# Attention with hash buckets and a soft mixture of experts: another start-up and other emission times

## Chip, cores and metric

The kernel runs on one core of one Trainium2 chip. The metric is the device time of one execution in microseconds (us). Engines are TensorE (PE, with its weight loads as PEld), VectorE (DVE), ScalarE (ACT), GpSimd (POOL) and SyncE (SP), whose queue issues most transfers.

## What is computed

Four batches of eight heads, 768 positions, 64 columns a head. Every position of q and of k gets a bucket number from the signs of six projections; a score counts only where the buckets agree. What the attention gives goes through a soft mixture of eight experts with four slots each.

```python
q_bits = (np.einsum('bhsd,dk->bhsk', q, proj) > 0)      # k_bits alike
mask   = q_bucket[:, :, :, None] == k_bucket[:, :, None, :]
scores = np.where(mask, scale * np.matmul(q, k.T), -1e9)
attn   = np.exp(scores - np.max(scores, -1, keepdims=True))
attn   = attn / (np.sum(attn, -1, keepdims=True) + 1e-09)
x      = attn @ v                       # then, over (B*S, H*D):
logits = x @ phi                        # dispatch weights: softmax over rows
slot_out = relu(slot_input @ w1) @ w2   # combine weights: softmax over slots
out    = c @ slot_out
```

## The kernel before, in words

**One head.** A tile `XY` holds, on 128 partitions, what the scores of a head are multiplied from: rows 0 to 63 the high part of q and k, rows 64 to 95 the bits and a row of shifts, rows 96 to 127 the low parts. Three such tiles take turns (the names XY_134, XY_135 and XY_136 in the rows are heads 0, 1 and 2, then again). `smax` (L395) multiplies rows 0 to 95 for a first estimate of each row's maximum: 12 pieces a head, which fill nine PSUM tiles, two of them at a time (`p_sm`), and DVE reduces each (L409, L412). `shift` and `shift_rows` (L422 to L441) turn the maxima, ACT casts them (L440), and SP sends them into row 64 of the head's tile (`XY<-mr`). Only then can `scores` (L444) multiply all 128 rows; ACT takes the exponential of each of the nine `st` tiles (L457). POOL adds the exponentials up (`acc`, L464 and L470), and `av` (L472) multiplies them with v.

**A pair of heads.** q and k of two heads come in one load each (`load`, L200: `stage<-qk`, 384 KB each, two of them). `split_hi` (ACT, L307) and `split_lo` (POOL L317 for the first two pairs, then DVE L314) cut them into parts, `bits` (L356) multiplies by the projections and `over` (L347) compares. The `spread_` functions (L324 to L391) copy these into the `XY` tiles with DMAs inside the chip, through SP. The `pair_` functions sum, invert and turn what two heads give; `batch_` functions do the same for eight heads.

**The order.** Nothing is scheduled by a tool: `at` (L754) gives each step a number from the tables ONCE and STEADY (numbers count tiles, 6 a head and 12 a pair; a STEADY number holds for every pair), the steps are sorted by it, and each engine runs its own instructions in the order in which the steps then record them. A pair takes 12 slots, so a slot of the table is a twelfth of a pair's time. Each engine waits only for its own next instruction: what stands behind a waiting one waits too, on SP as well.

**The start.** Before head 0 can begin, `first_bits` (L364) casts q and k, multiplies bits and compares them in four pieces, two of q and then two of k (DVE, L348 through `over`). TensorE is kept at work in between: `keep_warm` (L250) multiplies constants, and `spin` (L416) is a filler of 64 rows by 512 columns of head 0's own tile, four ahead of the first maxima (`at(spin, 4)`) and two after each of head 0's nine maxima (L414).

**The end.** Expert weights are loaded by `load_weights` at numbers of the tables and, in the last 14 slots, as buffers come free; the experts follow behind the last head (from L866).

Of the kernel before, what the change touches and what calls it, by code (L numbers as in the profile page):

```python
# [18 lines left out]
P = 128  # L19
# [26 lines left out]
    ('acc', 0, 0): 3.585914, ('acc', 0, 1): 4.22685, ('acc', 0, 2): 5.524667, ('acc', 1, 0): 8.946979,  # L46
    ('acc', 1, 1): 10.956391, ('acc', 1, 2): 12.344873, ('av', 0, 0): 5.054363, ('av', 0, 1): 5.478537,
    ('av', 0, 2): 5.757673, ('av', 1, 0): 9.710007, ('av', 1, 1): 10.255163, ('av', 1, 2): 11.214499,
# [3 lines left out]
    ('pair_add', 0): 17.755806, ('pair_log', 0): 17.093498, ('pair_rec', 0, 0): 16.439496,  # L52
    ('pair_rec', 0, 1): 17.493222, ('pair_rec', 0, 2): 17.06204, ('pair_sum', 0): 14.253612,
    ('pair_turn', 0): 15.311115, ('pair_x', 0, (0, 1)): 20.048062, ('pair_x', 0, (2,)): 17.817429,
    ('scores', 0, 0, 0): 0.168486, ('scores', 0, 0, 1): 1.125661, ('scores', 0, 1, 0): 1.223956,
    ('scores', 0, 1, 1): 0.33384, ('scores', 0, 2, 0): 2.334467, ('scores', 0, 2, 1): 2.987076,
    ('scores', 0, 3, 0): 3.245695, ('scores', 0, 3, 1): 0.44555, ('scores', 0, 4, 0): 3.495737,
    ('scores', 0, 4, 1): 2.875345, ('scores', 0, 5, 0): 3.003256, ('scores', 0, 5, 1): 4.099239,
    ('scores', 1, 0, 0): 6.858146, ('scores', 1, 0, 1): 5.870022, ('scores', 1, 1, 0): 5.92247,
    ('scores', 1, 1, 1): 6.192369, ('scores', 1, 2, 0): 8.409656, ('scores', 1, 2, 1): 7.415615,  # L60
    ('scores', 1, 3, 0): 7.420621, ('scores', 1, 3, 1): 8.585449, ('scores', 1, 4, 0): 8.877145,
    ('scores', 1, 4, 1): 8.735371, ('scores', 1, 5, 0): 8.835046, ('scores', 1, 5, 1): 7.918247,
    ('shift', 0): -3.784083, ('shift', 1): 2.753538, ('shift_rows', 0): -2.475046, ('shift_rows', 1): 4.45141,
    ('smax', 0, 0, 0): -5.130492, ('smax', 0, 0, 1): -8.590815, ('smax', 0, 1, 0): -7.560504,
    ('smax', 0, 1, 1): -7.539257, ('smax', 0, 2, 0): -8.690095, ('smax', 0, 2, 1): -6.037478,
    ('smax', 0, 3, 0): -5.866639, ('smax', 0, 3, 1): -5.350979, ('smax', 0, 4, 0): -3.977164,
    ('smax', 0, 4, 1): -4.372204, ('smax', 0, 5, 0): -4.147594, ('smax', 0, 5, 1): -6.133271,
    ('smax', 1, 0, 0): 0.789461, ('smax', 1, 0, 1): -2.662486, ('smax', 1, 1, 0): -2.516273,
    ('smax', 1, 1, 1): 0.351061, ('smax', 1, 2, 0): 0.154013, ('smax', 1, 2, 1): 2.575717,
    ('smax', 1, 3, 0): 2.715207, ('smax', 1, 3, 1): 0.080615, ('smax', 1, 4, 0): 2.254769,  # L70
    ('smax', 1, 4, 1): -3.276176, ('smax', 1, 5, 0): -2.661486, ('smax', 1, 5, 1): 1.386723,
    ('split_hi', 0): -19.520063, ('split_lo', 0, 0): -13.277774, ('split_lo', 0, 1): -14.899121,
    ('spread_bits', 0): -12.730307, ('spread_bits', 1): -6.105477, ('spread_l', 0): -3.252795,
    ('spread_l', 1): -6.507778, ('spread_x', 0): -6.522482, ('spread_x', 1): -2.692262, ('spread_y', 0): -12.855738,
    ('spread_y', 1): -7.587243,
# [17 lines left out]
    ('load_weights', 6): 88.324917, ('load_weights', 7): 94.440496, ('load_weights', 8): 100.324917,
    ('load_weights', 9): 106.440496, ('one_add', 30): 190.865, ('one_add', 31): 193.725, ('one_fold', 3): 189.99,
    ('one_log', 30): 188.431, ('one_log', 31): 193.7, ('one_put', 30): 191.5, ('one_put', 31): 195.722,
    ('one_rec', 30): 190.86, ('one_rec', 31): 192.8, ('one_sum', 30): 189.395, ('one_sum', 31): 191.0,
    ('one_turn', 30): 189.777, ('one_turn', 31): 192.0, ('one_x', 30): 191.23, ('one_x', 31): 193.72,
    ('scores', 10, 0, 1): 61.076546, ('scores', 12, 0, 1): 73.076546, ('scores', 14, 0, 1): 85.076546,
    ('scores', 16, 0, 1): 97.076546, ('scores', 18, 0, 1): 109.076546, ('scores', 20, 0, 1): 121.076546,
    ('scores', 3, 2, 0): 20.32086, ('scores', 5, 2, 0): 32.32086, ('scores', 6, 0, 1): 37.076546,  # L100
    ('scores', 7, 2, 0): 44.32086, ('scores', 8, 0, 1): 49.076546, ('scores', 9, 2, 0): 56.32086,
    ('shift_rows', 0): -3.190102, ('smax', 1, 0, 0): 1.271144, ('smax', 1, 0, 1): 1.233474,
    ('smax', 1, 1, 0): 1.270655, ('smax', 1, 1, 1): -2.856536, ('smax', 1, 2, 0): -1.78673,
    ('smax', 1, 2, 1): -0.694624, ('smax', 1, 3, 0): -0.199892, ('smax', 1, 3, 1): 0.329768,
    ('smax', 1, 4, 0): 0.343642, ('smax', 1, 4, 1): -2.830546, ('smax', 1, 5, 0): -2.805791,
    ('smax', 1, 5, 1): -2.024059, ('spin', 0): -35.655358, ('split_hi', 2): -28.475173, ('split_lo', 0, 0): -33.5,
    ('split_lo', 0, 1): -32.0, ('split_lo', 2, 0): -28.344955, ('split_lo', 2, 1): -3.110769,
    ('spread_bits', 1): -29.5, ('spread_bits', 2): 0.979704, ('spread_l', 0): -33.0, ('spread_l', 1): -3.111769,
    ('spread_l', 2): 3.432598, ('spread_x', 0): -31.0, ('spread_x', 1): -21.308377, ('spread_x', 2): 9.432814,
    ('spread_y', 1): -34.0, ('spread_y', 2): 0.523129, ('spread_y', 25): 136.325917, ('spread_y', 27): 148.325917,  # L110
    ('spread_y', 29): 160.325917, ('spread_y', 3): 4.325917, ('spread_y', 31): 172.325917,
# [35 lines left out]
def lsh_attention_soft_moe(  # L147
# [61 lines left out]

    eps = cp.tile([P, 1], F32, name="eps")  # L210
# [3 lines left out]
    ones = cp.tile([P, 32], F32, name="ones")  # L214
    nc.vector.memset(ones, 1.0)
    idle = pts[2][:, 0:P]
    nc.vector.memset(idle, 1.0)
# [145 lines left out]

    def first_bits():  # L364
        w = parts_of(0)
        bt = st[0]["bt"] = st[1]["bt"] = pp.tile([P, HC], F32R, name="bt", bufs=1)
        for x in range(2):
            pt = p_st.tile([P, 512], F32, name="st")
            bits_of(0, x, pt)
            nc.scalar.copy(Ys[0][0:64, x], raw[0:64, x])  # L370
            if x == 0:
                nc.scalar.copy(w[:, 0], raw[:, 0])
            for j in (2 * x, 2 * x + 1):
                over(Ys[0][64:80, x, (j % 2) * HC:(j % 2 + 1) * HC], pt, slice(32 * j, 32 * j + 16))
            if x:
                nc.scalar.copy(pts[0][0:64, 0:HC], before[0:64, 0:HC])
                nc.scalar.copy(w[:, 2], raw[:, 1])
                nc.scalar.copy(pts[0][64:128, 0:HC], pt[64:128, 0:HC])
            before = pt
# [681 lines left out]
```

## Time and profile before

| what | value |
|---|---|
| three runs | 494.96, 500.72, 505.84 us (median 500.72) |
| the profiled execution | 495.73 us, of which the span of its instructions is 493.9 us |
| busy share of the span | PE 97%, PEld 60%, DVE 74%, ACT 50%, POOL 67% |
| mean granted TensorE clock | 0.97 of full speed |
| chain that ended last | PE 87%, DMA 9%, DVE 1% |
| DMA | 99.71 MB, mean 202 GB/s |

The table is one execution. A stretch of the span is read from the time at which the first instruction named in it starts. The full clock is 2.4 GHz; where a row says 0.50, the granted one is 1.2 GHz.

### The profile page before, as it was taken

How to read it: one execution, taken by the hardware profiler on the slowest of the kernel's cores; microseconds unless marked ns; L12 is line 12 of the kernel's file. 1: busy time of each engine (PE TensorE's matmuls, PEld its weight loads, DVE VectorE, ACT ScalarE, POOL GpSimd, SP SyncE). 2: the span in 40 equal slices, each digit the busy share in tenths (PEclk: the TensorE clock that was granted, in tenths of full speed). 3: DMA queues.
4: the chain of work that ended last, by engine and by line, in shares of the span. 5: the costliest groups of instructions: out<-in, count | busy, mean ns of one | idle time of the engine just before them, and what ended most of it. 6: DMA issues, size and time to landing. Idle time of an engine off the chain costs nothing.

```text
span 493.9 us, 10762 instructions
## 1 busy us (share of the span) xinstructions
PE 477.1 (97%) x4047; PEld 298.8 (60%) x4047; DVE 367.1 (74%) x690; ACT 246.3 (50%) x465; POOL 331.1 (67%) x236
## 2 busy tenths in 40 slices
PE   8999999799999999999999999999999999989992
PEld 6466666465666566656566666666666665553581
DVE  3466888487989897978899988888889866463242
ACT  5127464345566546554666464646565544531251
POOL 8619686578777796868677968686779687702200
PEclk9569999899999999999999999999999999999997
DMA  6646675848575756676775777767767578999967
GB/s 153 152 117 153 164 165 151 200 93 225 119 224 122 202 141 165 180 209 178 195 188 170 191 209 183 208 178 212 181 184 173 153 171 286 376 353 406 409 248 286
DMA packets 39696, 99.71 MB, mean 202 GB/s; under 512 B 7422, under 2 KB 13708, under 8 KB 39644
## 3 DMA queue, kind: packets, MB, share of 16 engines
q1 hardware_dynamic: 39260, 98.16, 69.0%
q0 software_dynamic: 224, 0.47, 0.4%
q8 instruction: 32, 0.52, 0.4%
q10 hardware_dynamic: 160, 0.39, 0.3%
q14 instruction: 20, 0.16, 0.1%
HBM read 52.76 MB, written 6.29 MB: 120 GB/s over the span
## 4 chain that ended last, share of the span: by engine, by line
PE 87%; DMA 9%; DVE 1%; SPq 0%; issue 0%; ACT 0%; DVEq 0%; ACTq 0%
PE st L453 27%; PE av L482 22%; PE smx L406 15%; DMA XY<-mr 5%; PE qs L974 3%; PE qh L892 3%; DMA stage<-qk 2%; PE mi L494 2%; PE mi L544 2%; PE mi L353 2%; PE av L420 2%; DMA w<-w 2%; PE mi L509 1%; PE mi L529 1%; PE mi L699 1%; PE qa L937 1%
## 5 line engine op out<-in xcount | busy, mean ns | idle before, releaser
L470 POOL TENSOR_TENSOR acc<-acc,pt 128x768 f32<-128x768 f32 x125 | 229.2, 1833 | 37.1 <-ACT pt L457 29.5
L457 ACT ACTIVATE pt<-st 128x512 f32<-128x512 f32 x288 | 162.4, 596 | 57.5 <-PE st L453 50.3
L453 PE MATMUL st<-XY 128*128 128x512 f32 (+1 forms) x768 | 172.0, 345 | 4.3 <-DMA XY<-mr 4.2
L412 DVE TENSOR_REDUCE mx<-smx 128x1 f32<-128x512 f32 x192 | 130.4, 687 | 36.2 <-PE smx L406 33.7
L482 PE MATMUL av<-pt,v 128*32 128x384 f32 x1536 | 137.0, 488 | 0.0
L453 PEld LDWEIGHTS st<-XY 128*128 128x128 f32 x768 | 121.9, 192 | 19.5 <-DMA XY<-mr 5.6
L406 PE MATMUL smx<-XY 96*128 96x512 f32 (+1 forms) x384 | 124.2, 372 | 0.5 <-DVE mx L412 0.5
L464 POOL TENSOR_TENSOR acc<-pt 128x768 f32<-128x768 f32 x32 | 58.8, 1837 | 49.9 <-ACT pt L457 49.7
L406 PEld LDWEIGHTS smx<-XY 96*128 96x128 f32 x384 | 69.8, 195 | 33.0 <-DVE mx L412 8.3
L482 PEld LDWEIGHTS av<-pt,v 128*32 128x32 f32 x1536 | 46.6, 110 | 67.6 <-issue 66.7
L409 DVE TENSOR_REDUCE mx<-smx 128x2 f32<-128x512 f32 x96 | 63.8, 677 | 11.4 <-PE smx L406 10.7
L486 ACT COPY avs<-av 128x384 f32<-128x384 f32 x32 | 15.3, 478 | 93.9 <-PE av L482 93.9
L314 DVE TENSOR_REDUCE stage<-stage 128x768 fp32r<-128x1536 f32 x28 | 50.2, 1792 | 1.0 <-ACT pt L457 0.4
L501 DVE RECIPROCAL sm<-sm 128x128 f32<-128x128 f32 x45 | 39.7, 912 | 0.0
L546 DVE TENSOR_TENSOR xq<-mi,r 128x256 f32<-128x256 f32 x45 | 17.5, 418 | 24.3 <-PE mi L544 24.3
L307 ACT ACTIVATE stage<-stage 128x768 fp32r<-128x768 f32 x30 | 24.5, 839 | 17.8 <-DMA stage<-qk 12.9
L544 PEld LDWEIGHTS mi<-ident,avs 128*128 128x128 f32 x90 | 10.5, 141 | 11.4 <-issue 9.4
L974 PE MATMUL qs<-w 128*32 128x128 f32 (+1 forms) x360 | 15.8, 305 | 0.0
L544 PE MATMUL mi<-ident,avs 128*128 128x128 f32 x90 | 15.6, 281 | 0.0
L931 POOL CAST avs<-lacc 128x48 fp32r<-128x48 f32 x8 | 2.1, 268 | 19.5 <-ACT lacc L922 12.4
L892 PE MATMUL qh<-w,siT 128*32 128x512 f32 x128 | 14.6, 595 | 0.0
L353 PE MATMUL mi<-stage,pb 128*32 128x384 f32 x120 | 13.1, 510 | 0.0
(179 smaller groups left out, 346.6 us busy)
## 6 DMA issues: line engine op xcount, KB each, us to landing
w<-w SPq DMA_DIRECT2D x61, 512.0 KB
XY<-stage SPq DMA_DIRECT2D x62, 384.0 KB
stage<-qk SPq DMA_DIRECT2D x32, 384.0 KB
XY<-stage SPq DMA_DIRECT2D x62, 192.0 KB
v<-vt SPq DMA_DIRECT2D x32, 192.0 KB
out<-w SPq DMA_DIRECT2D x12, 512.0 KB
xq<-w SPq DMA_DIRECT2D x3, 512.0 KB
XY<-bt SPq DMA_DIRECT2D x62, 19.5 KB
```

Of the source, the lines that this page charges most:

```text
L314: nc.vector.tensor_reduce(out=w[:, 2 * x + 1], in_=stage[:, x:n + 1:n - x].rearrange("p t s -> p s t"), axis=AX.X, op=ALU.add, negate=True)
L406: nc.tensor.matmul(pt[:, o:o + b - a], Ys[h % N_Y][0:96, 0, t * P:(t + 1) * P], Ys[h % N_Y][0:96, 1, a:b], start=True, stop=True)
L409: nc.vector.tensor_reduce(out=mx[:, n - 1:n + 1], in_=pt.rearrange("p (a x) -> p a x", a=2), axis=AX.X, op=ALU.max)
L412: nc.vector.reduce_max(out=mx[:, n:n + 1], in_=pt, axis=AX.X)
L453: nc.tensor.matmul(pt[:, o:o + b - a], x[:, 1, i * P:(i + 1) * P], x[:, 0, a:b], start=first, stop=not first)
L457: nc.scalar.activation(pts[i // 2][:, 512 * u:512 * u + 512], pt, AF.Exp, scale=D ** -0.5)
L464: nc.gpsimd.tensor_tensor(out=s["acc"], in0=pr[:, 0:S], in1=pr[:, S:2 * S], op=ALU.add)
L470: eng.tensor_tensor(out=s["acc"], in0=s["acc"], in1=pr[:, a * S:(a + 1) * S], op=ALU.add)
L482: nc.tensor.matmul(s["av"][D * c + d:D * c + d + 32, 0:HC], s["v"][:, i, d:d + 32], pr[:, o + c * HC:o + (c + 1) * HC], start=(i == 0), st ...
L501: nc.vector.reciprocal(out=rs[:, k * P:(k + 1) * P], in_=rs[:, k * P:(k + 1) * P])
L544: nc.tensor.transpose(pt[:, o:o + P], st[h + a]["avs"][:, k * P:(k + 1) * P], ident)
L974: nc.tensor.matmul(po[32 * j:32 * j + 32], hTs[g][:, f, 32 * j:32 * j + 32], wt[1, x, 2 * g + f // 4, j].rearrange("p (f m) -> p f m", f=4 ...
```

## The change

1. The start: the two memsets that the first constant matmuls need go to the front of DVE. SP issues k, then the constants with the projections, then q (before: constants, q, k).
2. `first_bits` works on k first. Of the four comparisons three stand ahead of the first maximum (both of k, the first of q); the fourth, with the two copies out of PSUM, is a step of its own (`first_last`) behind it.
3. Fillers: `spin` covers 96 rows in place of 64 and is issued once in place of twice behind each maximum of head 0; the four ahead of them are gone; `keep_warm` ahead of them goes from 14 to 3.
4. New numbers for nearly all steps, in both tables.

```diff
-    def load(h):
-        for x in range(2):
+    def load(h, xs=(0, 1)):
+        for x in xs:
             nc.sync.dma_start(out=raw[:, x], in_=qk[x, h // 2])
...
+    load(0, (1,))
     nc.sync.dma_start(out=pre[:, 0:C_ID + 64], in_=first[:, 0:C_ID + 64])
-    load(0)
+    load(0, (0,))
...
+    def first_over(x, c):
+        j = 2 * x + c
+        over(Ys[0][64:80, x, c * HC:(c + 1) * HC], first_pt[x], slice(32 * j, 32 * j + 16))
+
     def first_bits():
         w = parts_of(0)
-        for x in range(2):
-            pt = p_st.tile([P, 512], F32, name="st")
-            bits_of(0, x, pt)
-            nc.scalar.copy(Ys[0][0:64, x], raw[0:64, x])
-            if x == 0:
-                nc.scalar.copy(w[:, 0], raw[:, 0])
-            for j in (2 * x, 2 * x + 1):
-                over(Ys[0][64:80, x, (j % 2) * HC:(j % 2 + 1) * HC], pt, slice(32 * j, 32 * j + 16))
...
+        for x in (1, 0):
+            first_pt[x] = p_st.tile([P, 512], F32, name="st")
+            bits_of(0, x, first_pt[x])
+            nc.scalar.copy(Ys[0][0:64, x], raw[0:64, x])
             if x:
                 nc.scalar.copy(w[:, 2], raw[:, 1])
+                first_over(1, 0)
+                first_over(1, 1)
+        first_over(0, 0)
+        nc.scalar.copy(w[:, 0], raw[:, 0])
+
+    def first_last():
+        first_over(0, 1)
+        nc.scalar.copy(pts[0][64:128, 0:HC], first_pt[1][64:128, 0:HC])
+        nc.scalar.copy(pts[0][0:64, 0:HC], first_pt[0][0:64, 0:HC])
...
         if h == 0 and n % 4 != 1:
-            spin(2)
+            spin(1)
...
-        y = Ys[0][0:64, 0]
+        y = Ys[0][0:96, 0]
...
-    at(keep_warm, 14, True, tag="a")
+    at(keep_warm, 3, True, tag="a")
     at(copy_ident)
     at(first_bits)
+    at(first_last)
...
-    at(spin, 4, tag=0)
...
-    ('bits', 0): -13.111727, ('load', 0): -19.876778, ('load_v', 0): 0.438592, ('load_v', 1): 6.200893,
+    ('bits', 0): -13.641611, ('load', 0): -22.629268, ('load_v', 0): -2.150801, ('load_v', 1): 1.001645,
```

**TensorE at the start.** `av<-pt_84` are the constant matmuls of `keep_warm`, `st<-stage` the bits of head 0, `av<-XY_134` the fillers, `smx<-XY_134` the pieces of head 0's maxima. Before:

```order
L254 MATMUL av<-pt_84,ones 32x128 x7
L353 MATMUL st<-stage,pb 32x384 x4
L254 MATMUL av<-pt_84,ones 32x128 x14
L420 MATMUL av<-XY_134 128x512 x4
L406 MATMUL smx<-XY_134 128x512
L420 MATMUL av<-XY_134 128x512 x2
L406 MATMUL smx<-XY_134 128x256 x2
```

After the change:

```order
L258 MATMUL av<-pt_84,ones 32x128 x7
L357 MATMUL st<-stage,pb 32x384 x4
L258 MATMUL av<-pt_84,ones 32x128 x3
L418 MATMUL smx<-XY_134 128x512
L432 MATMUL av<-XY_134 128x512
L418 MATMUL smx<-XY_134 128x256 x2
L432 MATMUL av<-XY_134 128x512
```

Fifteen matmuls fewer stand between the bits and the first piece of a maximum, and one filler in place of two behind each piece.

**SP's queue around the row of maxima of head 5** (`XY_136<-mr`), the third pair of heads. `w<-w` are expert weights, `stage<-qk` the loads of a later pair, `XY<-stage` and `XY<-bt` copies inside the chip. Before:

```order
L293 DMA v_88<-vt 128x384
L189 DMA w<-w 128x1024 x2
L202 DMA stage<-qk 128x768 x2
L321 DMA XY_135<-stage 64x2x768
L321 DMA XY_136<-mr 1x12x128
L321 DMA XY_134<-stage 64x2x768
```

After the change:

```order
L297 DMA v_89<-vt 128x384
L205 DMA stage<-qk 128x768 x2
L192 DMA w<-w 128x1024 x2
L325 DMA XY_136<-mr 1x12x128
L325 DMA XY_135<-stage 64x2x768
L325 DMA XY_135<-bt 13x384 x2
```

The copy of 64 by 2 by 768 now stands behind the row of maxima, the loads of q and k stand ahead of the weights, and a load of v comes right ahead of these; the later pairs have the same order with one weight load.

**POOL in a pair of the steady stretch.** `acc` are the sums of a head's exponentials, out of the three buffers pt_82, pt_83 and pt_84; `lacc` is the sum of the pair before's logits. Before:

```order
L464 TENSOR_TENSOR acc_86<-pt_82 128x768
L470 TENSOR_TENSOR acc_86<-acc_86,pt_83 128x768 x2
L470 TENSOR_TENSOR acc_86<-acc_86,pt_84 128x768 x2
L523 TENSOR_TENSOR lacc<-lacc,sm 128x384
L464 TENSOR_TENSOR acc_87<-pt_82 128x768
```

After the change:

```order
L476 TENSOR_TENSOR acc_86<-pt_82 128x768
L482 TENSOR_TENSOR acc_86<-acc_86,pt_83 128x768 x2
L535 TENSOR_TENSOR lacc<-lacc,sm 128x384
L482 TENSOR_TENSOR acc_86<-acc_86,pt_84 128x768 x2
L476 TENSOR_TENSOR acc_87<-pt_82 128x768
```

The sum of logits has moved ahead of the last two sums of exponentials.

## Rows read from the trace of the kernel before

**Rows 1.** Busy time by stretch: length, five engines, granted clock, DMA share, GB/s.

```profile
10.75:25.19 14.44, 14.44 (x31) 6.69 (x30) 6.22 (x9) 2.98 (x4) 9.90 (x9) 0.60 0.64 146
...
48.88:73.42 24.54, 24.54 (x208) 15.75 (x211) 20.99 (x37) 13.49 (x26) 18.36 (x11) 1.00 0.67 165
73.42:103.07 29.65, 26.37 (x208) 17.04 (x211) 21.21 (x37) 13.58 (x26) 19.27 (x12) 0.94 0.72 174
103.07:128.40 25.33, 24.80 (x207) 15.78 (x211) 20.81 (x37) 13.58 (x26) 19.30 (x12) 1.00 0.63 162
...
203.62:228.54 24.92, 24.82 (x208) 15.81 (x211) 21.15 (x37) 13.61 (x26) 19.32 (x12) 1.00 0.69 192
228.54:253.76 25.22, 24.81 (x208) 15.80 (x211) 21.16 (x37) 14.00 (x27) 18.00 (x12) 1.00 0.71 184
...
328.97:353.50 24.53, 24.53 (x207) 15.74 (x211) 21.44 (x37) 13.94 (x27) 18.02 (x12) 1.00 0.72 197
...
432.11:441.74 9.63, 8.37 (x93) 4.91 (x94) 6.16 (x25) 2.72 (x8) 0.04 (x1) 1.00 0.95 376
```

**Rows 2.** The chain that ended last, start and us, at the start.

```profile
10.82 0.43 PE smx L406
11.25 0.66 PE av L420 x2
...
21.83 0.72 PE smx L406 x2
22.55 1.15 PE av L420 x2
...
44.31 0.47 PE st L453 x2
...
44.78 0.24 PE smx L406
```

**Rows 3.** Instructions in order of time, all engines, 0 to 31 us: start, us.

```profile
6.10 2.76 DVE L348 TENSOR_SCALAR XY<-st,con 16x384 fp32r<-16x384 f32 x4 [3.19 <-PE st L353]
...
10.75 0.50 PE L406 MATMUL smx<-XY 96*128 96x512 f32 x1
...
11.29 0.69 DVE L412 TENSOR_REDUCE mx<-smx 128x1 f32<-128x512 f32 x1 [2.43 <-PE smx L406]
...
18.09 0.84 ACT L307 ACTIVATE stage<-stage 128x768 fp32r<-128x768 f32 x1 [1.33 <-DMA stage<-qk]
...
25.19 0.17 DVE L427 TENSOR_REDUCE mi<-mx 128x6 f32<-128x12 f32 x1
...
25.50 1.51 PE L353 MATMUL mi<-stage,pb 128*32 128x384 f32 x8
...
27.46 0.26 ACT L440 CAST mr<-mi 12x128 fp32r<-12x128 f32 x1 [8.52 <-PE mi L437]
27.74 0.81 SPq L321 DMA_DIRECT2D XY<-mr  x1
...
30.80 0.63 PE L453 MATMUL st<-XY 128*128 128x512 f32 x1
```

**Rows 4.** Instructions in order of time, SP and TensorE, 82 to 95 us.

```profile
82.63 0.85 SPq L202 DMA_DIRECT2D stage<-qk  x2
...
85.64 0.69 SPq L321 DMA_DIRECT2D XY<-stage  x1
...
86.71 0.77 SPq L321 DMA_DIRECT2D XY<-mr  x1
...
94.83 0.74 PE L453 MATMUL st<-XY 128*128 128x256 f32 x4 [3.28 <-DMA XY<-mr]
```

**Rows 5.** Instructions in order of time, POOL and DVE, 340 to 350 us.

```profile
340.85 7.58 POOL L470 TENSOR_TENSOR acc<-acc,pt 128x768 f32<-128x768 f32 x4 [1.67 <-ACT pt L457]
...
344.79 0.56 DVE L521 TENSOR_TENSOR sm<-mi,sm 128x384 f32<-128x384 f32 x1
...
348.39 1.02 POOL L523 TENSOR_TENSOR lacc<-lacc,sm 128x384 f32<-128x384 f32 x1
```

More of the change, by code (lines that the diff above doesn't have):

```diff
@@ L53 @@
[L53 to L58, printed above, removed]
@@ new lines @@
+    ('pair_add', 0): 17.577879, ('pair_log', 0): 16.993927, ('pair_rec', 0, 0): 15.693025,
+    ('pair_rec', 0, 1): 15.7677, ('pair_rec', 0, 2): 15.521381, ('pair_sum', 0): 14.239421,
+    ('pair_turn', 0): 15.346973, ('pair_x', 0, (0, 1)): 20.437414, ('pair_x', 0, (2,)): 17.890042,
+    ('scores', 0, 0, 0): 0.095393, ('scores', 0, 0, 1): 1.201587, ('scores', 0, 1, 0): 2.467216,
+    ('scores', 0, 1, 1): 0.576418, ('scores', 0, 2, 0): 0.194762, ('scores', 0, 2, 1): 2.954077,
+    ('scores', 0, 3, 0): 3.066209, ('scores', 0, 3, 1): 2.808786, ('scores', 0, 4, 0): 2.713342,
@@ new lines @@
+    ('scores', 0, 4, 1): 3.452949, ('scores', 0, 5, 0): 4.612255, ('scores', 0, 5, 1): 0.740437,
+    ('scores', 1, 0, 0): 6.224469, ('scores', 1, 0, 1): 6.596277, ('scores', 1, 1, 0): 6.933339,
+    ('scores', 1, 1, 1): 6.295257, ('scores', 1, 2, 0): 7.197935, ('scores', 1, 2, 1): 7.034394,
+    ('scores', 1, 3, 0): 7.126508, ('scores', 1, 3, 1): 9.279904, ('scores', 1, 4, 0): 9.595666,
+    ('scores', 1, 4, 1): 8.443296, ('scores', 1, 5, 0): 9.009943, ('scores', 1, 5, 1): 7.777135,
+    ('shift', 0): -3.732058, ('shift', 1): 2.981046, ('shift_rows', 0): -2.48744, ('shift_rows', 1): 4.460206,
@@ new lines @@
+    ('load', 10): 37.688669, ('load', 12): 49.688669, ('load', 14): 61.688669, ('load', 2): -12.762070462,
+    ('load', 4): 3.305061249, ('load', 6): 13.688669, ('load', 8): 25.688669, ('load_phi',): 10.931086823,
+    ('load_v', 0): -61.78673, ('load_weights', 0): 26.669343, ('load_weights', 1): 27.9087,
+    ('load_weights', 10): 111.216379, ('load_weights', 11): 119.361725, ('load_weights', 12): 123.216379,
+    ('load_weights', 13): 131.361725, ('load_weights', 14): 135.216379, ('load_weights', 15): 143.361725,
@@ new lines @@
+    ('one_add', 30): 190.865, ('one_add', 31): 193.725, ('one_fold', 3): 189.99, ('one_log', 30): 188.431,
+    ('one_log', 31): 193.7, ('one_put', 30): 191.5, ('one_put', 31): 195.722, ('one_rec', 30): 190.86,
+    ('one_rec', 31): 192.8, ('one_sum', 30): 189.395, ('one_sum', 31): 191.0, ('one_turn', 30): 189.777,
+    ('one_turn', 31): 192.0, ('one_x', 30): 191.23, ('one_x', 31): 193.72, ('scores', 10, 0, 1): 61.396684,
+    ('scores', 12, 0, 1): 73.396684, ('scores', 14, 0, 1): 85.396684, ('scores', 16, 0, 1): 97.396684,
@@ new lines @@
+    ('scores', 18, 0, 1): 109.396684, ('scores', 20, 0, 1): 121.396684, ('scores', 3, 2, 0): 19.21665,
+    ('scores', 5, 2, 0): 31.21665, ('scores', 6, 0, 1): 37.396684, ('scores', 7, 2, 0): 43.21665,
+    ('scores', 8, 0, 1): 49.396684, ('scores', 9, 2, 0): 55.21665, ('shift_rows', 0): -3.614750908,
+    ('smax', 0, 0, 0): -48.201477503, ('smax', 1, 0, 0): -0.414889731, ('smax', 1, 0, 1): -0.455916355,
+    ('smax', 1, 1, 0): -0.415889731, ('smax', 1, 1, 1): -2.391596163, ('smax', 1, 2, 0): 1.521154004,
@@ L207, in lsh_attention_soft_moe @@
     vs = [held.tile([P, NT, D], F32, name=f"v{i}") for i, held in enumerate((ap, mp))]
+    ones = cp.tile([P, 32], F32, name="ones")
+    nc.vector.memset(ones, 1.0)
+    idle = pts[2][:, 0:P]
+    nc.vector.memset(idle, 1.0)
     eps = cp.tile([P, 1], F32, name="eps")
```

96 lines of the change are left out of this document (36 added, 60 removed).

## The prediction, made before the changed kernel ran

> **What bounds the kernel now.** I read the page's shares first (TensorE busy 97% of the span, mean granted clock 0.97), then busy time by stretch, the chain that ended last, and the order of time where the chain leaves TensorE or where the change works. By stretch [rows 1] a pair of heads takes 24.53 or 24.54 us and TensorE is busy in all of it; VectorE has some 3 us to spare there. So in the steady stretch TensorE sets the time, and an order of the same matmuls can hardly win. Time to be won lies where TensorE waits or does filling work:
>
> - The start. Head 0's maxima fill 10.75 to 25.19, 14.44 us for nine reductions, at a mean granted clock of 0.60. The chain shows why [rows 2]: it runs through TensorE's pieces and fillers, not through VectorE. At 10.8 us a piece takes 0.43 us and two fillers 0.66; at 22 us, at the low clock (1.2 GHz), 0.72 and 1.15, 1.87 a step, while a reduction is 0.69 [rows 3]. The fillers are 61% of a step.
> - Four pairs that take longer than 24.54: 29.65, 25.33, 24.92 and 25.22 [rows 1], together 6.96 us more. In the largest the row of maxima is issued at 86.71 and TensorE's first score starts at 94.83 after 3.28 us idle, released by that row [rows 4]; afterwards the clock is low for a while (mean 0.94 of the stretch, busy 26.37 in place of 24.54).
>
> **The change part by part.** All sums are made against the profiled execution, 495.73 us (span 493.9 and 1.83 around it). It lies 5.0 below the median of the three runs, 500.72, and near the lowest.
>
> *Ahead of the first piece.* Now four comparisons run from 6.10 for 2.76 us, 0.69 each, and the first piece starts at 10.75 [rows 3], behind fillers. After the change k and the constants come first, in the place of constants and q: the same bytes, so the bits of k are ready about when those of q are now. Three comparisons end at 6.10 + 3 x 0.69 = 8.17, and the fillers that remain (three constant matmuls) are over by then. The first piece starts near 8.3: 2.4 us won (2.0 to 2.7, as k lands a little later or earlier). The memsets moved on VectorE are worth under 0.1.
>
> *The nine maxima.* The lower end is VectorE's: 0.54 from the first piece to its reduction (11.29 less 10.75), nine reductions and the fourth comparison at 0.69, and some 0.5 because the second filler reads what that comparison writes and the third piece stands behind it: 0.54 + 10 x 0.69 + 0.5 = 7.9. The upper end keeps the low clock and today's cost of a filler: 9 x (0.72 + 1.15 / 2) + 0.5 = 12.2. Between them I take 8.8, nearer to the lower: the 0.43 at full clock is 0.2 more than the 0.235 of each of two scores, and of a piece between scores (0.47 for two, 0.24 for one [rows 2]), so the extra belongs to the change between 64 and 96 rows, which goes. Then 14.44 becomes 8.8, 5.6 won, and the maxima end near 8.3 + 8.8 = 17.1 in place of 25.19.
>
> *What is late next.* The cast of the row of maxima is behind the casts of the second pair's q and k on ACT, and the bits of that pair (four matmuls, in rows 25.50 and 1.51 us [rows 3]) stand ahead of head 1's pieces on TensorE. Both need the second k, which lands at 18.09 now [rows 3]; ACT is free of it at 18.93. So of the 8.0 won so far a part is given back. From the bits at 25.50 to the first score at 30.80 is 5.30 us now, and the row issued at 27.74 has landed by then. With k no earlier the first score stands at 18.09 + 5.30 = 23.4, 7.4 won. One copy of ACT's (32 x 2 x 768 numbers, 0.20 MB, 1.35 us at the 146 GB/s of this stretch [rows 1]) has gone behind the cast of the row. If half of that was ahead of k, the score stands at 22.7, 8.1 won. Bounds: 6.4 (k a microsecond later) to 9.0 (the clock is full and the bits save 0.8 too). I take 8.0. The Trainium skill, DMA: Bandwidth & Descriptors, "Issuing engines are not separate DMA queues", says that transfers from any engine run on the same DMA engines and interleave; by it that copy does count against the load, and without it 7.4 would stand.
>
> What head 1 and head 2 need next is issued in the same order behind this and has slack: SP's transfers for them follow the row at once.
>
> *The row of maxima in the steady stretch.* Ahead of it on SP stands now a copy of 64 x 2 x 768 numbers, 0.39 MB, issued at 85.64, about a microsecond before the row [rows 4]; at the 165 to 174 GB/s of these stretches [rows 1] it takes some 2.3 us. It goes behind the row. That alone is more than the excess of three of the four long pairs (0.79, 0.38, 0.68) and 2.3 of the 5.11 of the first. The loads of q and k, now issued at 82.63, four microseconds ahead, get a number 2.75 slots lower, 2.75 x 24.54 / 12 = 5.6 us earlier, as far as SP's queue allows, which takes the rest. Against it, a load of v (0.20 MB) is now in front. The bounds are 0 won and 6.96; I take 6.0, as the trace has the row late by less than the copy in three cases of four.
>
> *The rest of the steady order.* The matmuls are the same in number and shape. TensorE has no idle time in an undisturbed pair, which hides the moves on VectorE, ACT and POOL; cover can be lost (third rival). I cost it at 0, with 0.2 us a pair either way, 3 us over 15 pairs. The end, with its wait for weights (432.11 to 441.74, DMA share 0.95 [rows 1]), is issued in slots counted from the last head and moves with the loop.
>
> Sum: 495.73 - 8.0 - 6.0 = 481.7, say **482 us**.
>
> **The rivals.**
>
> *The row of maxima stays late.* For it: the change puts weights, v, q and k (about 2 MB) straight ahead of the row; at 376 GB/s, the best rate in these rows, they need 5.3 us, and the runs spread over 11 us, more than the 7 us of waits in the trace. Against it: all of these were ahead of the row before too, and the copy is gone. Then only the start is won: 495.73 - 8 = 488, and 493 with the median run's 5 us more.
>
> *The clock stays low and the fillers cost what they do now.* Fillers are there to hold the clock; the trace lost it with twice as many, while TensorE was busy 14.44 of 14.44 us [rows 1], so halving them cannot be counted on to hold it. The maxima then take 12.2 and the start wins 2.4 + 2.2 = 4.6, with k no longer the last. 495.73 - 4.6 - 6 = 485. The Trainium skill, TensorE: Matmul & The Clock Gate, "Part 1: The HAM clock gate", says that the slow state is the default and activity releases it; by that rule fewer fillers mean more of the slow clock, and this is where it would lead. The stretch at 0.60 does not contradict it.
>
> *POOL comes late (slower).* The sum of logits now stands ahead of the last two sums of exponentials. In the trace the four sums run 340.85 to 348.43, and the logits' product, which POOL's sum waits for, ends at 345.35 on VectorE [rows 5]. Moved ahead, POOL does two sums to 344.6, waits to 345.4, adds 1.02, and ends the other two (1.9 each) at 350.2, 1.7 us later than now. Those two free the buffer pt_84 for the next head's exponentials; beyond that ACT waits, then TensorE, whose three score buffers fill. POOL idles in the pair (18.0 to 19.3 busy of 24.5 [rows 1]) and so catches up, and the exponentials have about a microsecond before TensorE feels them. From a product some 2 us later than now each further microsecond is paid in 11 or 12 pairs. To be slower than 495.73 it must eat 14 us, 1.2 a pair; at 2 us a pair, 482 + 24 = 506. Against it: VectorE's slack.
>
> **How the numbers follow.** Forecast 0.62 (477 to 487), the late row 0.22 (486 to 494), the low clock 0.11 (483 to 488), POOL 0.05 (500 to 510). The range for 8 in 10 reaches from 476 (start 9.0, waits 7.0, order 3 better) to 494. About 2% is what a measurement of this kernel can tell from no change, 490.7 against the median. The forecast gives 0.58 of its 0.62 to faster (against a run of before near 495 it could be less than 2%), the late row half, 0.11, the low clock 0.09, together 0.78; POOL gives 0.04 to slower; the rest, 0.18, is within 2%.
>
> **What would show it right or wrong.** The first piece of a maximum near 8.3; nine reductions with little idle time on VectorE, ending near 17; ACT's second cast of the new k as the last thing ahead of the row's cast; the first score near 22.8. Undisturbed pairs all at 24.5, no wait of TensorE for the row of maxima, DMA's share of the chain down from 9%. Wrong: a first score behind 26, waits for the row of over 3 us in all, pairs of over 25, or ACT waiting for POOL's sums in every pair.

## The result, and the profile after

The changed kernel takes **482.3 us** (median of four runs, 480.1 to 482.8) against 499.1 us before (median of four, 495.0 to 505.8): ratio 0.968, 95% interval 0.960 to 0.976. It is faster, and the prediction was 482, 476 to 494. The profiled execution took 480.1 us, span 478.4. Some executions of a kernel are over 1.5% longer than its fastest, at a lower granted clock: ratios here leave them out, medians do not, and no trace of one is read.

The page of the kernel after: busy shares, and the chain that ended last by engine.

```profile
PE 461.8 (97%) x4012; PEld 290.6 (61%) x4012; DVE 364.4 (76%) x690; ACT 250.3 (52%) x465; POOL 330.5 (69%) x236
...
PE 90%; DMA 2%; POOL 2%; DVE 2%; issue 1%; ACT 1%; SPq 1%; DVEq 0%; ACTq 0%; POOLq 0%
```

TensorE's share is what it was, over a span that is 15.5 us shorter: waits and fillers went together. Transfers, 9% of the chain before, are 2%.

Busy time by stretch after: head 0's maxima, the third pair of heads, and in the last row 14 pairs together (PEclk is TensorE's granted clock as a share of full speed).

```profile
core 0: us, PE busy (x) PEld busy (x) DVE busy (x) ACT busy (x) POOL busy (x), PEclk, DMA share, GB/s
7.93:15.99 8.06, 6.53 (x21) 4.44 (x21) 6.80 (x10) 3.24 (x5) 7.91 (x8) 0.79 0.86 217
...
64.33:88.91 24.58, 24.58 (x204) 15.75 (x203) 20.91 (x37) 13.64 (x26) 18.94 (x12) 1.00 0.76 200
...
39.78:388.73 348.95, 348.95 (x2900) 222.93 (x2899) 300.03 (x529) 197.99 (x366) 272.87 (x164) 1.00 0.70 181
```

The same 14 pairs before:

```profile
48.81:404.12 355.31, 350.99 (x2901) 224.48 (x2900) 301.63 (x529) 194.35 (x366) 272.89 (x164) 1.00 0.68 177
```

Against [rows 1]: the nine maxima take 8.06 us where they took 14.44. The pair that took 29.65 takes 24.58, and the other three long ones are down to 24.6 too; TensorE is busy in all of the 348.95 us. (Every fourth pair, three of the 14, takes 26.1 us in both kernels: 26.12 before, 26.13 to 26.18 after.)

For the rest of the document the span is cut in three: the *start*, up to the first matmul of head 1's weighted sums (48.8 us before, 39.8 after), the *14 pairs* from there to the same matmul of head 29 (355.3 before, 348.95 after), and the *end*, 89.8 and 89.7. The gain of 15.5 us is 9.0 in the start and 6.4 in the pairs.

The start after, in order of time, all engines (rows of before: [rows 3]).

```profile
5.18 1.38 DVE L352 TENSOR_SCALAR XY<-st,con 16x384 fp32r<-16x384 f32 x2 [0.94 <-PE st L357]
...
7.12 0.67 DVE L352 TENSOR_SCALAR XY<-st,con 16x384 fp32r<-16x384 f32 x1 [0.56 <-PE st L357]
...
8.44 0.69 DVE L424 TENSOR_REDUCE mx<-smx 128x1 f32<-128x512 f32 x1 [0.65 <-PE smx L418]
...
8.85 3.59 POOL L321 TENSOR_TENSOR stage<-stage 128x768 fp32r<-128x768 f32 x2
...
12.58 1.65 POOL L352 TENSOR_SCALAR bt<-pt,con 128x384 fp32r<-128x384 f32 x1
...
14.25 3.29 SPq L325 DMA_DIRECT2D XY<-bt  x4
...
17.42 0.84 ACT L311 ACTIVATE stage<-stage 128x768 fp32r<-128x768 f32 x1 [1.74 <-DMA stage<-qk]
...
18.43 0.77 SPq L325 DMA_DIRECT2D XY<-mr  x1
...
19.01 0.70 PE L418 MATMUL smx<-XY 96*128 96x512 f32 x2 [0.73 <-DMA XY<-bt]
...
22.14 1.91 PE L465 MATMUL st<-XY 128*128 128x512 f32 x4
```

Two comparisons run at 5.18, the third waits 0.56 us for q's bits, the first reduction starts at 8.44 (11.29 before), and the last ends at 15.95. Then TensorE waits for the copies of head 1's bits, which come by way of GpSimd's low parts and comparison; the first score starts at 22.14 (30.80 before).

SP's queue after, at the place of [rows 4].

```profile
72.09 0.90 SPq L205 DMA_DIRECT2D stage<-qk  x2
73.03 1.99 SPq L192 DMA_DIRECT2D w<-w  x2
76.99 0.76 SPq L325 DMA_DIRECT2D XY<-mr  x1
77.85 0.71 SPq L325 DMA_DIRECT2D XY<-stage  x1
78.61 3.48 SPq L325 DMA_DIRECT2D XY<-bt  x4
```

The row of maxima, then the copy that stood ahead of it, then the bits, now ahead of all other copies. TensorE's waits after hold no line for the row of maxima. Before, in the 14 pairs, they held this one (us in total, times, longest):

```profile
PE st L453 <- DMA XY<-mr: 4.2, 3, 3.3
```

GpSimd's sums in a late pair, which answer to [rows 5], and ScalarE's one wait for those sums:

```profile
280.68 1.00 POOL L535 TENSOR_TENSOR lacc<-lacc,sm 128x384 f32<-128x384 f32 x1 [0.43 <-DVE sm L533]
281.64 3.75 POOL L482 TENSOR_TENSOR acc<-acc,pt 128x768 f32<-128x768 f32 x2
...
ACT pt L469 <- POOL acc L482: 0.3, 1, 0.3
```

GpSimd waits 0.43 us for VectorE's product (L533), adds it and ends the sums at 285.39; ScalarE waits for them 0.3 us in the whole execution.

### The profile page after: what moved, and what is told of

Its sections match the earlier page's. It is cut to its first block, busy times and chain, and to the rows that moved or that the text cites. A ratio compares the mean times of both kernels' runs of the same rounds, so it can differ in the third digit from the quotient of the medians.

```text
span 478.4 us, 10738 instructions
## 1 busy us (share of the span) xinstructions
PE 461.8 (97%) x4012; PEld 290.6 (61%) x4012; DVE 364.4 (76%) x690; ACT 250.3 (52%) x465; POOL 330.5 (69%) x236
## 4 chain that ended last, share of the span: by engine, by line
PE 90%; DMA 2%; POOL 2%; DVE 2%; issue 1%; ACT 1%; SPq 1%; DVEq 0%; ACTq 0%; POOLq 0%
PE st L465 29%; PE av L494 27%; PE smx L418 15%; PE qh L904 3%; PE mi L556 3%; PE mi L506 2%; PE mi L521 2%; PE qs L986 2%; PE mi L357 2%; DMA out<-w 1%; PE mi L541 1%; PE mi L711 1%; PE qa L949 1%; POOL stage L321 1%; PE mi L449 1%
## 5 line engine op out<-in xcount | busy, mean ns | idle before, releaser
L469 ACT ACTIVATE pt<-st 128x512 f32<-128x512 f32 x288 | 164.1, 596 | 49.0 <-PE st L465 41.0
L465 PE MATMUL st<-XY 128*128 128x512 f32 (+1 forms) x768 | 180.1, 346 | 0.0
L465 PEld LDWEIGHTS st<-XY 128*128 128x128 f32 x768 | 129.5, 190 | 16.3 <-issue 0.6
L418 PE MATMUL smx<-XY 96*128 96x256 f32 (+1 forms) x384 | 117.8, 360 | 1.6 <-DMA XY<-bt 0.7
L418 PEld LDWEIGHTS smx<-XY 96*128 96x128 f32 x384 | 68.7, 191 | 29.6 <-DVE mx L424 8.8
L421 DVE TENSOR_REDUCE mx<-smx 128x2 f32<-128x512 f32 x96 | 64.8, 675 | 4.3 <-PE smx L418 3.8
L513 DVE RECIPROCAL sm<-sm 128x128 f32<-128x128 f32 x45 | 38.1, 896 | 0.0
L509 ACT ACTIVATE sm<-mi,eps 128x384 f32<-128x384 f32 x15 | 8.7, 582 | 13.8 <-PE mi L506 13.8
L986 PE MATMUL qs<-w 128*32 128x128 f32 (+1 forms) x360 | 15.5, 305 | 0.0
```

The lines of the kernel that those rows point to most:

```text
L418: nc.tensor.matmul(pt[:, o:o + b - a], Ys[h % N_Y][0:96, 0, t * P:(t + 1) * P], Ys[h % N_Y][0:96, 1, a:b], start=True, stop=True)
L421: nc.vector.tensor_reduce(out=mx[:, n - 1:n + 1], in_=pt.rearrange("p (a x) -> p a x", a=2), axis=AX.X, op=ALU.max)
L465: nc.tensor.matmul(pt[:, o:o + b - a], x[:, 1, i * P:(i + 1) * P], x[:, 0, a:b], start=first, stop=not first)
L469: nc.scalar.activation(pts[i // 2][:, 512 * u:512 * u + 512], pt, AF.Exp, scale=D ** -0.5)
L513: nc.vector.reciprocal(out=rs[:, k * P:(k + 1) * P], in_=rs[:, k * P:(k + 1) * P])
```

## The experiments

All twelve compute the whole output; only orders and fillers differ. Times are medians of the runs, ratios are against before in the same session. The cut into start and pairs is that of each profiled execution, one per kernel. The second has a time only.

| kernel | time, us | ratio (95%) | start | 14 pairs |
|---|---|---|---|---|
| before | 496.7 to 501.7 by session | 1 | 48.8 | 355.3 |
| after | 482.3 | 0.968 (0.960 to 0.976) | 39.8 | 349.0 |
| 1 before, copy behind the row | 499.2 | 1.003 (0.999 to 1.007) | 46.9 | 358.0 |
| 2 before, loads early | 500.0 | 0.999 (0.994 to 1.004) | | |
| 3 after, copy ahead of the row | 488.2 | 0.980 (0.973 to 0.986) | 40.2 | 357.9 |
| 4 after, loads late | 481.6 | 0.966 (0.959 to 0.973) | 39.3 | 351.2 |
| 5 before, row, copy, bits | 502.9 | 1.013 (1.004 to 1.021) | 48.2 | 362.2 |
| 6 after, bits behind | 499.7 | 1.008 (1.006 to 1.011) | 41.0 | 367.3 |
| 7 after, GpSimd reordered | 484.2 | 0.974 (0.966 to 0.982) | 43.6 | 351.1 |
| 8 the same, second pair's bits late | 486.1 | 0.978 (0.972 to 0.985) | 44.4 | 350.0 |
| 9 before, all of SP's times of after | 491.3 | 0.990 (0.982 to 0.998) | 49.5 | 349.9 |
| 10 after, two fillers of 64 rows | 488.8 | 0.985 (0.975 to 0.994) | 46.5 | 351.1 |
| 11 after, no fillers | 482.6 | 0.973 (0.965 to 0.981) | 40.7 | 349.9 |
| 12 after, GpSimd and bits in waits | 483.3 | 0.969 (0.963 to 0.976) | 41.6 | 350.8 |

### What took the waits out of the pairs

**Experiment 1**, in before:

```diff
-('spread_y', 1): -7.587243
+('spread_y', 1): -7.54
```

> The kernel before with one edit: the copy of the upper rows of an odd head's operand (spread_y, 0.39 MB) is sent just behind the row of maxima of the preceding pair, not just ahead of it. What is asked: which half of the change took the 6.96 us of waits for that row out of the pairs. Theory C (the copy standing ahead of the row on SP's queue is what makes it late): most of the 6.96 us go, the pair from 73.42 to 103.07 comes down from 29.65 to below 26 us, and PE's waits on the transfer of mr (9.8 us in the profile of before) fall under 3 us; the execution takes about 489.5 us against 495.7. Theory L (the loads of q and k, 0.79 MB, still under way when the row is issued, make it late): the row gains at most the copy's 2.3 us, the long pair stays over 27 us, 493 to 495 us.

TensorE's waits in its pairs, in order of their totals (us, times, longest):

```profile
PE smx L406 <- DMA XY<-bt: 3.0, 3, 1.3
...
PE st L453 <- DMA XY<-mr: 0.3, 1, 0.3
```

The 9.8 us named ahead of it add TensorE's 4.2 and 5.6 of its weight loads for the same row, so 4.2 is what 0.3 compares with. The long pair came down, to 26.0 us, and the waits for the row went, as theory C said. The time did not: most other pairs are now some tenths longer (24.5 to 26.1, and 26.7 to 27.2 for every fourth), and the first maxima of the next head wait for their bits, whose copies the moved copy has pushed back. One wait was traded for another.

**Experiment 2**, in before: `('load', 0): -19.876778` to `-22.629268`, and the loads of heads 6 to 14 by 2.7.

> The kernel before with the other half alone: the loads of the next pair's q and k are issued 2.75 slots (5.6 us) earlier, as in the kernel after; the copy stays ahead of the row. Theory L: the row of maxima finds a free queue, all but 1 us of the 6.96 us go, pairs of 24.6 us, about 489.5 us. Theory C: the row still waits behind the copy, the long pair stays near 28 to 29 us, 493 to 495 us. If both halves alone bring about all of it, either lead is enough, and the sum of the prediction had no need of both.

No gain that can be measured; theory L, as a sufficient cause, falls.

**Experiment 3**, in after:

```diff
-('scores', 0, 5, 0): 4.612255
+('scores', 0, 5, 0): 4.455
-('spread_y', 1): -6.537259
+('spread_y', 1): -7.5425
```

> The kernel after with the copy of the odd head's upper rows sent ahead of the row of maxima again (for that the last scores of the earlier head move some 0.16 slots forward, ahead of the turn of the maxima, which costs two half-wide matmuls of delay, under 0.3 us a pair and hidden if the row has slack). The loads stay early. Theory C: waits for the row come back, PE's wait on mr over 4 us in total, 485 to 489 us. Theory L: no wait over 1 us comes back, 480 to 483 us.

SP's queue in the long pair, and TensorE's wait:

```profile
78.81 0.71 SPq L325 DMA_DIRECT2D XY<-stage  x1
79.70 0.78 SPq L325 DMA_DIRECT2D XY<-mr  x1
...
PE st L465 <- DMA XY<-mr: 5.8, 3, 3.4
```

5.8 us of waits are back and the pairs are 9.0 us longer, all of it in three of them (1.7, 2.2 and 5.1); the others are within 0.2 of those of after, so the moved scores cost nothing. By the medians it is 5.9 us. So the copy's place costs what the prediction's step gave it, when the rest of the queue is that of after. **Experiment 4**, in after, the loads where before had them:

> The kernel after with the loads of q and k issued 2.75 slots later, where the kernel before had them. The copy stays behind the row. Theory L: waits for the row or for the parts of k come back, above all in pairs with two pieces of weights, 4 to 6 us, 484 to 488 us. Theory C: nothing changes beyond 1 us, 480 to 483 us.

The pairs are 2.2 us longer and the time is that of after: the loads' lead is worth little.

**Experiment 5**, in before: the edit of experiment 1, and `('spread_bits', 1): -6.105477` to `-7.535`.

> The kernel before with the copy of the upper rows behind the row of maxima, as in the first experiment, and the four copies of the comparison bits (bt) moved up to just behind that copy, ahead of the three copies of parts, the order on SP's queue that the kernel after has. Theory Q (each copy in the queue costs its place: the first experiment traded a late row for late bits, and only an order with the row first and the bits second has neither): the pairs come down from 25.4 us on average to under 25.0, no wait over 1 us for mr or bt is left, execution 487 to 491 us. Theory P (the gain in the pairs comes from the new order on TensorE itself, the maxima and scores placed elsewhere; the queue only moved which of two waits is named): the pairs stay at 25.2 us or more, 494 us and above.

```profile
PE av L482 <- DMA v<-vt: 11.6, 11, 2.2
...
PE st L453 <- DMA XY<-mr: 1.1, 1, 1.1
```

Those rows are TensorE's waits. Row and bits are in time but for 1.1 us, and now v is late, eleven times, up to 2.2 us. The change loads v 2.6 and 5.2 slots earlier; this run didn't. By its numbers (25.9 us a pair, 502.9 us) it came out as theory P has it; by its waits it did as the first, and handed the wait on. **Experiment 6**, in after:

```diff
-('spread_bits', 1): -5.559256
+('spread_bits', 1): -5.515
-('spread_l', 1): -2.707075
+('spread_l', 1): -5.516
```

> The kernel after with the copies of the bits of an odd head moved behind the copies of parts (two for the head's x, one for its low parts), the place that they had before; the row of maxima stays first. Theory Q: the first maxima of the next head wait for their bits, 0.3 to 1.3 us in most pairs as in the first experiment, 484 to 493 us. Theory P: TensorE's new order needs the bits later or not at all sooner than they come, 480 to 483 us.

At 499.7 us it is beyond what either theory allowed. Theory P falls: one place in the queue for the bits is 17 us of time. (For it the copy of the low parts came 2.8 slots forward; the maxima read rows 0 to 95 and so not the low parts.) SP, TensorE and VectorE in a pair whose weighted sums of the odd head start at 105.20:

```profile
105.84 4.54 SPq L325 DMA_DIRECT2D XY<-stage  x4
110.42 3.31 SPq L325 DMA_DIRECT2D XY<-bt  x4
...
114.84 0.17 DVE L439 TENSOR_REDUCE mi<-mx 128x6 f32<-128x12 f32 x1
...
115.03 0.36 PE L418 MATMUL smx<-XY 96*128 96x256 f32 x1 [0.49 <-DVE mi L439]
```

The same in the kernel after, where those sums start at 277.06:

```profile
278.47 3.47 SPq L325 DMA_DIRECT2D XY<-bt  x4
...
286.24 0.29 PE L418 MATMUL smx<-XY 96*128 96x256 f32 x1
...
286.70 0.17 DVE L439 TENSOR_REDUCE mi<-mx 128x6 f32<-128x12 f32 x1
```

The wait is put down to VectorE's L439. But in the kernel after the same maxima start at 286.24, before L439 begins at 286.70, so they don't need it. What differs is the bits: sent 5.2 us after the sums begin, where the kernel after sends them at 1.4 us. This is the case in which a wait's named releaser is only the event nearest in time.

**Experiment 9** puts theory Q to the test as a whole: before, with every steady time from after that decides SP's queue (`load`, `load_v`, `load_weights`, `spread_y`, `spread_l`, `spread_x`, `spread_bits`), and nothing else.

> The kernel before with every emission time of the steady part that decides SP's queue taken from the kernel after: loads of q and k, of v and of the weights, and the copies of upper rows, parts and bits; TensorE, VectorE, ScalarE and GpSimd keep the order of before, the start too. Theory Q (the order of the whole queue is what took the waits out of the pairs; any single piece moved alone only hands the wait on, as three runs here showed): 14 pairs sum to 349 to 351.5 us as in the kernel after (355.3 before), execution 487.5 to 491 us. Theory P (TensorE's new order is needed with it): a wait for another transfer or for VectorE takes its place and the pairs sum to 354 us or more, 493 us and above.

```profile
49.51:399.37 349.86, 349.19 (x2900) 223.29 (x2899) 301.52 (x529) 195.14 (x366) 272.94 (x164) 1.00 0.70 180
```

That is the row of the 14 pairs: 349.9 us against 355.3 before and 349.0 after, with TensorE's old order. Theory Q holds, with the time at 491.3, 0.3 above its range: SP's queue alone makes the pairs what they are, and none of the pieces tried did (the copy, the loads, copy and bits). v and the weights were not moved alone.

### What made the start short

**Experiment 10**, in after: `spin(2)` for `spin(1)` and `Ys[0][0:64, 0]` for `Ys[0][0:96, 0]`.

> The kernel after with the fillers between head 0's maxima as before: two of 64 rows behind each instead of one of 96. Theory F (at the low clock a step costs TensorE its two or three matmuls, and a change between 64 and 96 rows costs extra): nine maxima take near 14 us in place of 8.06, end near 21.9 us, first score near 27.2, 487.4 us. Theory W (the denser work holds TensorE's clock up, so three matmuls a step cost about 1 us): nine maxima near 10 us, and the 3 us that they had to spare before the bits of head 1 arrive cover most of it, 482 to 484 us.

TensorE's order of time in it: two steps at the low clock, and the first score.

```profile
14.18 0.79 PE L418 MATMUL smx<-XY 96*128 96x512 f32 x1
14.90 1.22 PE L432 MATMUL av<-XY 64*128 64x512 f32 x2
16.05 0.79 PE L418 MATMUL smx<-XY 96*128 96x512 f32 x1
...
27.72 1.91 PE L465 MATMUL st<-XY 128*128 128x512 f32 x4
```

A step is 1.87 us (16.05 less 14.18), as before at 22 us, and the first score is 5.6 us later. In the kernel after, at the same low clock, piece and filler take 0.86: 0.43 each. Theory F holds. The run changes the number of fillers and their rows together, so what a change of rows costs is read from the weight loads (PEld). A filler and the load for the next piece, in the kernel after:

```profile
11.17 0.63 PE L432 MATMUL av<-XY 96*128 96x512 f32 x1
...
11.40 0.28 PEld L418 LDWEIGHTS smx<-XY 96*128 96x128 f32 x1
```

The load for the piece of 14.18 in experiment 10:

```profile
14.18 0.29 PEld L418 LDWEIGHTS smx<-XY 96*128 96x128 f32 x1 [0.65 <-DVE mx L424]
```

In the kernel after the load runs under the filler ahead of it. In experiment 10 load and matmul begin together, and so again at 14.90; the reduction that the row names had ended 0.35 us earlier, so it is not what held the load. Two loads of 0.29 stand open in a step, and three matmuls at 0.43 are the rest of the 1.87. Two fillers of 96 rows were not tried. **Experiment 11** leaves the fillers out (`spin(1)` to `pass`):

> The kernel after without any filler behind head 0's maxima. Theory F: TensorE is no limit any more, VectorE's nine reductions of 0.69 us are, the maxima end near 15 us instead of 15.99; the bits of head 1 still come at 19.0, so the first score stays near 22 and the time at 482 us within 1. Theory W: without fillers the clock is low from the maxima on into head 1's maxima and the first scores: each 512-column matmul there takes 0.43 us instead of 0.24, 2 to 4 us more, 484 to 486 us.

The first score starts at 22.35, head 0's maxima end at 15.8 and the time is that of after within its runs, as theory F has it. The clock did what theory W has it do. From the end of head 0's maxima to the first score, in the kernel after, in experiment 11, and in experiment 12 below, which has the fillers:

```profile
15.99:22.14 6.15, 3.93 (x16) 1.73 (x16) 3.71 (x8) 0.99 (x2) 5.60 (x5) 0.91 0.56 129
...
15.81:22.35 6.54, 5.20 (x15) 2.36 (x16) 3.73 (x8) 0.99 (x2) 5.28 (x5) 0.50 0.59 135
...
15.65:22.84 7.19, 5.58 (x15) 2.27 (x16) 3.76 (x8) 1.95 (x3) 4.49 (x4) 0.62 0.52 128
```

Without fillers the clock is at 1.2 GHz in all of that stretch; in the kernel after it is full in most of it. TensorE waits there for over a third of the time in the kernel after (busy 3.93 of 6.15 us), so the lower clock cost little: the first score is 0.2 us later and the start 1.0 us longer (40.7 for 39.8), not 2 to 4. That the fillers hold the clock isn't shown either, since experiment 12 has them and lost it too, and each row is one execution. The Trainium skill, TensorE: Matmul & The Clock Gate, "Part 1: The HAM clock gate", says that the slow state is the default and activity releases it. Experiment 11's row agrees with that; head 0's maxima before, at 0.60 with TensorE busy in 14.44 of 14.44 us [rows 1], do not, and there the measurement decides: busy fillers did not hold the clock.

### What ends last at the start now

**Experiment 7**, in after: `('split_lo', 0, 1)` and `('split_lo', 0, 0)` to -90 and -89, the rows of ones (`first_rows`, 1) and the identity to -37.3 and -37.25.

> The kernel after with GpSimd's work at the start in another order: the low parts of the first k and q and the bits of heads 0 and 1 (L321, L352) ahead of the copies of the rows of ones (L325) and of the identity. What is asked: what ended last at the start. Theory G (GpSimd's chain, splits then bits then four copies, ends last, at 19.01 us where the first maxima of head 1 start; the second pair's k is no limit): the bits go out near 12.3 us in place of 14.25, head 1's maxima start near 17.1, the first score comes near 20.3 in place of 22.14, execution 480.3 us against 482.3. Theory K (the second pair's k, 17.42, ends last as the prediction had it: TensorE's matmuls of the second pair's bits stand ahead of head 1's maxima and can't start before it lands): head 1's maxima start no sooner than 18.3, the first score no sooner than 21.4, 481.6 us.

GpSimd and SP in it, in order of time:

```profile
10.11 1.65 POOL L352 TENSOR_SCALAR bt<-pt,con 128x384 fp32r<-128x384 f32 x1 [0.68 <-ACT pt L391]
11.73 1.18 POOL L325 DMA_DIRECT2D XY<-XY  x2
...
17.45 3.29 SPq L325 DMA_DIRECT2D XY<-bt  x4
```

Neither theory: the bits were ready at 11.8, but their copies write into rows that the copies of L325 fill first, and waited for these until 17.45. The start became 3.8 us longer. The second pair's k, asked for by 10.14, landed at 15.55 in this run, so 17.42 isn't fixed. **Experiment 8** adds `('bits', 2)` to -0.41 and `('split_hi', 2)` to -3.55:

> The same, and what hangs on the second pair's q and k moved back: the matmuls of its bits behind five of head 1's maxima (all the bits' matmuls on TensorE), and the casts of its high parts (L311) behind the cast of the first row of maxima on ScalarE. Theory K: with nothing of the second pair ahead of it, the row goes out near 17.3 in place of 18.43 and the first score comes near 20.3, about 1.1 us before the run without this edit; 480.4 us. Theory G: no gain over that run. A third outcome, that the row itself lands late behind the bits' copies, would leave the first score near 21 with a wait for mr in front of it.

The bits went out at 17.31, so the question that it asked of the second pair stayed hidden behind the same wait; the first score came at 26.94 against 25.81, with the second pair's bits (1.51 us) now ahead of it. **Experiment 12** keeps L325 in its place: `('split_lo', 0, 1)` to -90, `copy_ident` to -37.25, `('bits', 2)` to -3.65.

> The kernel after with both things that stand between head 0's maxima and head 1's moved into waits: on GpSimd the low part of k in the 2.2 us in which it waits for the row of ones, the copies L325 where they were, the cast of the identity last (the run with GpSimd reordered lost time since the bits' copies wait for those of L325); and on TensorE the second pair's bits ahead of the turn of head 0's maxima, into its wait of 1.3 us. Theory G: the bits of heads 0 and 1 go out near 12.1 us in place of 14.25 and land near 16.9, the second pair's k is asked for earlier (its buffer is read by then) and lands near 15.7; head 1's maxima start near 17.2 in place of 19.01, the first score comes near 20.3 in place of 22.14, about 480.4 us against 482.3. Theory K (the second pair's k sets the pace whatever is done on GpSimd): k lands at 17 or later, the turn of the maxima waits behind it, and the first score stays at 22 or later, 482 us or more.

SP, ScalarE and TensorE in order of time:

```profile
10.48 1.55 SPq L205 DMA_DIRECT2D stage<-qk  x2
12.54 3.78 SPq L325 DMA_DIRECT2D XY<-bt  x4
...
17.54 0.84 ACT L311 ACTIVATE stage<-stage 128x768 fp32r<-128x768 f32 x1 [0.40 <-DMA stage<-qk]
17.56 1.50 PE L357 MATMUL mi<-stage,pb 128*32 128x384 f32 x4 [0.41 <-DMA stage<-qk]
...
22.84 1.91 PE L465 MATMUL st<-XY 128*128 128x512 f32 x4
```

The bits went out 1.7 us earlier. The loads were issued by 12.03, 0.8 us sooner than in the kernel after (10.68 and 2.11 us), and k still landed at 17.54. So theory K holds for this order: the turn of the maxima stood behind the second pair's bits, and head 1's maxima start at 19.12 (19.01 in the kernel after, 17.2 by theory G). The first score, at 22.84, is 0.7 us later than in the kernel after; 0.6 of that lies behind the start of those maxima (3.72 us against 3.13), where this execution has the lower clock. In the kernel after the second pair's bits' matmuls start at 17.02 and take 1.26, so with k where it is a shorter chain through GpSimd can win at most 0.7 us (19.01 less 18.28). The Trainium skill, DMA: Bandwidth & Descriptors, "Issuing engines are not separate DMA queues", has all transfers share the same engines and interleave. That fits: the bits' copies go out right behind the loads, the DMA share in head 0's maxima is 0.95 in this run, and the load that was asked for sooner landed no sooner. None of these versions beats the kernel after.

## Why the prediction was right, and where its steps were not

- *Ahead of the first piece*: 2.4 us were forecast, 8.3; measured 7.93, 2.8 won. q's bits came later than the step had them, the third comparison ended at 7.79, not 8.17, since the first two began at 5.18.
- *The nine maxima*: 8.8 forecast, 8.06 measured. The reading that the extra cost belongs to the change between 64 and 96 rows is borne out by experiment 10 and its weight loads. The upper bound, 9 x (0.72 + 1.15 / 2), was too high: without that change a step at the low clock is 0.86, near VectorE's 0.69, so the rival of the low clock was half right on the clock (it fell to 1.2 GHz at 11.2 and was full again by 14.2, 0.79 in the stretch) and wrong on its price. Its remark that the stretch at 0.60 does not contradict the rule cited there was wrong: TensorE was busy in all of it (experiment 11). VectorE set the pace, as in the lower bound of 7.9: busy 6.80 of the 8.06.
- *What is late next*: 8.0 forecast for the start, 8.66 at the first score. It named the second k, forecast to land near 17.4, and it landed at 17.42. But the path was wrong: the last wait was for the bits of head 1, a chain through GpSimd that the step did not look at, 0.7 us behind what hangs on k. In experiment 12, with that chain shorter and the second pair's bits moved ahead of the turn, what hangs on k ends last.
- *The row of maxima*: 6.0 forecast, 6.4 measured, and the waits for it went. (Of the 6.96 that it calls waits, 4.3 were idle time of TensorE and 2.6 longer busy time, 1.8 of that in the stretch at 0.94.) Its explanation was half right. The copy must be behind the row (experiment 3), but "that alone" is not enough in before (experiment 1), and the loads' lead is worth little (experiments 2 and 4). The step missed the places of the bits and of v in the same queue (experiments 5, 6 and 9), which it had put into "the rest of the steady order" at 0. It came out right because the change moved the whole queue; for the step as argued that is luck.
- *The rest of the steady order*: undisturbed pairs are 24.55 to 24.61 in place of 24.53, within the 0.2 allowed. Experiment 9, with the old order on the other engines, has the same sum of pairs within a microsecond: the new order there is worth nothing that shows.
- *The rivals*: the row did not stay late, and GpSimd did not come late; its product came early enough that it waited 0.43 us, and ScalarE did not feel it.

That 482 met 482.3 is luck in part too. The gain forecast was 14.0 us; it was 15.6 between the profiled executions (495.73 to 480.13) and 16.8 between the medians. The sum set out from one of the faster executions of before, which made up for what it had too small.

Split by the profiled executions: of the start's 9.0 us the fillers between the maxima are 6.7 (46.5 in experiment 10 less 39.8), 5.6 of it by the first score and the rest behind it, where the clock was longer low. The other 2.3 are everything else at the start together: k first, three comparisons ahead, fewer constant matmuls and fillers ahead of the first piece, other orders on GpSimd and ScalarE. They were not taken apart. Of the pairs' 6.4 us SP's queue is 5.4 (355.3 less 349.9 in experiment 9), and the last microsecond is within what these sums vary by between runs that share an order (349.0 in the kernel after to 351.1 in experiments 7 and 10). Each of these is one execution; the ratio of experiment 9, 0.990, is of the same size.

## What to carry to other kernels

A queue of transfers that is issued in order is one resource: moving one transfer hands its wait to the next one, so judge an order as a whole, and test a single move in the new order as well as in the old. A filler should have the shape of the work beside it, or be left out where it does not show in the time. The clock of one execution is no property of an edit: look for a second execution of the same order before crediting it. Where two chains end within a microsecond, shortening one shows the other, and a gain there has to be sought in both.

## What the runs showed that was not expected

- At the low clock three matmuls of 512 columns in a row with a change between 64 and 96 rows took 1.87 us, and two of the same 96 rows 0.86: the two changes cost 1.87 - 3 x 0.43 = 0.58 us, which is two weight loads of 0.29 that nothing covered.
- In experiment 7 two copies of rows inside the chip, issued by GpSimd from 11.73 to 12.91, were waited for until 17.45: 4.5 us, while the DMA share was 1.01, 0.83 and then 0.16 (12 to 14, 14 to 16, 16 to 18 us). What held them through the last of these is open.
- The edit of experiment 6 (four copies behind three others, one of which came forward for it) cost 18.3 us in 14 pairs: 13.2 as idle time of TensorE (367.29 less its 354.12 busy) and 5.2 as longer busy time.
- TensorE's clock at the start differed between executions of one order. Experiment 4 has the start of the kernel after, instruction for instruction; its clock in head 0's maxima was 1.00 and they took 7.5 us, where the kernel after had 0.79 and 8.1. Experiment 12 had 1.00 and 7.3 us, experiment 11, without fillers, 0.79 and 7.7, and experiment 10, with two of 64 rows, 0.66 and 13.4. VectorE's reductions set the pace in all but the last, and there the clock mattered by about half a microsecond.
